# New order lists for the five engine queues of a fused attention and channel-mix kernel

## The chip, the cores and the metric

The kernel runs on one core of one Trainium2 chip. The metric is the device time of one execution in microseconds (us); lower is better. Runs are compared by their medians. The profile is one further execution, recorded instruction by instruction.

## The reference

Inputs are q, k and v of shape (8 batches, 8 heads, 576 tokens, 64), two mixing vectors and three weight matrices, all float32. The first half is causal attention in a window of 128 tokens with a linear penalty per head. Its result, laid out as (8, 576, 512), is x of the second half, a channel mix with a one-token shift.

```
scores = q @ k.T / 8 - slope[h] * (i - j),  only for 0 <= i - j < 128
x      = softmax(scores) @ v                        # then (batch, token, head*64 + d)
x_prev = x shifted by one token, zero at the start of a batch
xk     = mu_k * x + (1 - mu_k) * x_prev             # xr likewise with mu_r
k      = relu(xk @ w_k)                             # 512 -> 1024
out    = sigmoid(xr @ w_r) * ((k * k) @ w_v)        # 1024 -> 512
```

## The kernel before

The work is cut into 32 pairs of heads (8 batches of 4 pairs) for the attention, and into 4 pairs of batches (P = 0 to 3, 1152 tokens each) for the channel mix. Everything is written as named operations. The lists of names below (ORDER, from line 724) fix the order of the operations on each of five queues: PE (matmuls), ACT, DVE, POOL and SP. An engine takes its list in order: when one operation waits, all behind it on that engine wait too.

**Attention, pair n** (names end in the pair's number; pairs 0 to 3 are the first batch):

- `lql`, `lqp`, `lqn`, `lts` (POOL) load q and k; `lvs.b.j` loads V of batch b (j = 4 is the 64-token tail). `lts` loads the 64-token tails of q (0) and k (1). `lq` (SP) loads the first pair in float32.
- For batches 0 to 3, `ct` (DVE) reorders q and k by token, `tq` (PE) transposes them, `pq` (ACT) copies the result out of PSUM. The first pair has `c`, `tk` and `pk` as well. `tail` and `tcopy` do the same for the tails.
- For batches 4 to 7 the transposing is done by DMA instead: `tr.b.0` and `tr.b.1` (SP, line 92) cross all of q and of k of a batch, `trt` (line 97) its tails. `tr.b.i` needs the four loads `lqn.b.i.0` to `lqn.b.i.3`; the loads `lqn.(b+2).i.j` in turn go into the buffer that `tr.b.i` reads.
- `score.n.h` (PE, line 218) are the score matmuls of half h of the window, two heads side by side on 64 rows each. `exp` (ACT, line 226) takes the exponential, `mask` (DVE) multiplies by the window and penalty. The first four pairs add the penalty by an extra matmul (line 197) and have no `mask`.
- `av.n` (PE, line 249) multiplies by V and the row sum, `norm` (DVE, lines 260 and 261) divides, `ot` (PE) transposes back, `xt` (ACT) copies to the x tile. Pairs 0 to 3 do this in two halves, named `.0` and `.1`.
- `xk` and `xr` (DVE) make the two mixes.

**Channel mix, token chunks.** `m1.P.c0.f` (PE, line 312) is one 128-row slice f of xk @ w_k for the tokens from c0 on; a chunk has 256, 384 or 512 tokens. For two slices at the start it is split into `m1a` and `m1`. `rl` (ACT) is the relu, `kk` the square (DVE, twice in eight on ACT). `m3.P.c` (PE) is xr @ w_r for 128 tokens, `rs` (ACT) its gate. `m2a.P.c` and `m2.P.c` (PE) are the two halves of k*k @ w_v, `oo` (DVE) the product with the gate, `st` (SP) the store. The last two token blocks are split in columns instead (`oob`, `stb`). `lwk`, `lwr` and `lwv` (POOL) load the weights.

**Rings.** Tiles come from rings; an operation that takes a tile waits until the tile's users of one turn before are done. PSUM has a ring of 4 (`mm`: tq, tail, ot, m1, m3, m2a and the early av) and a ring of 2 (`sa`: scores and the later av). SBUF has 3 tiles for rl and 4 for the output product.

**Start.** `fill` are matmuls on zeros. `mask0` (ACT) computes the window mask, `mcopy` (DVE) copies it to its further places, `dcopy` and `sid` prepare the early pairs' penalty. `clear0`, `ms` and `clear` (POOL) are memsets: `clear0` for the first batch's V and k tails, `ms` for columns of the at and x tiles, `clear` for the other V buffers. The end is the last `oob` and `stb`.

How a list becomes dependences, and the crossbar with the planner's costs:

```
 568  op(("tr", b, i), "SP", 6800, lambda i=i: cross(b, i),
 569     [("lqn", b, i, j) for j in range(NF)] + old, n, land=9000)
 ...
 RINGS = {"sa": 2, "mm": 4, "ct": 3, "xu": 3, "dl": 4, "xm": 3, "xk": 2, "rl": 3,
          "kk": 2, "rs": 6, "ot": 4}
 ...
 for text in ORDER.values():
     line = [tuple(int(x) if x.isdigit() else x for x in w.split(".")) for w in text.split()]
     for a, o in zip(line, line[1:]):
         ops[o]["after"] = [a]
 plan()
```

`plan` emits the operations one after another; the `after` entries hold it to the lists. Its costs do not change what an engine executes or in which order.

Of the kernel before, what the change touches and what calls it, by code (L numbers as in the profile page):

```python
# [16 lines left out]
def kernel(  # L17
# [703 lines left out]
    for i, m in enumerate(FILL):  # L721
# [23 lines left out]
            m1.1.0.5 m1.1.0.7 av.15 m3.1.3 m3.1.0 score.19.1 score.19.0 ot.15 m1.1.0.3  # L745
            m3.1.1 m1.1.0.4 m1.1.0.1 m1.1.0.2 m1.1.512.0 m3.1.2 av.16 m1.1.512.5
            m2a.1.0 m1.1.512.3 m2a.1.2 m2.1.0 m1.1.512.4 av.17 av.18 m2.1.2 m1.1.512.1
            ot.16 m1.1.512.2 m1.1.512.6 m2a.1.3 score.21.1 score.20.1 m2.1.3 m3.1.6
            ot.18 score.22.1 score.22.0 m2a.1.1 ot.17 m2.1.1 av.19 m1.1.512.7 m3.1.5
            score.21.0 score.20.0 m3.1.8 m1.1.896.0 m3.1.4 m1.1.896.2 m3.1.7 ot.19  # L750
            score.23.0 score.23.1 m1.1.896.5 m1.1.896.7 m2a.1.6 m2a.1.4 m1.1.896.4
            m2.1.6 m2a.1.5 av.22 m2.1.4 m1.1.896.1 av.23 m2.1.5 ot.22 m1.2.0.0
            m1.1.896.3 m1.2.0.7 m1.2.0.1 av.20 m1.1.896.6 m1.2.0.6 m1.2.0.4 m1.2.0.3
            av.21 ot.20 m2a.1.8 m1.2.0.2 m2.1.8 ot.23 m3.2.1 m1.2.0.5 m3.2.0 ot.21
            m3.2.2 m2a.1.7 score.26.0 score.27.1 m2.1.7 m2a.2.0 m1.2.512.0 score.25.1
            score.24.1 m1.2.512.4 m2.2.0 m1.2.512.3 score.24.0 score.25.0 m3.2.3
            m1.2.512.6 score.26.1 score.27.0 m1.2.512.2 m1.2.512.7 m2a.2.3 m2a.2.1
            m2.2.3 m1.2.512.1 m2a.2.2 m2.2.1 m2.2.2 m1.2.512.5 m3.2.6 av.25 av.24
            m1.2.896.0 m3.2.4 av.27 m1.2.896.3 ot.24 m3.2.5 ot.27 ot.25 m1.2.896.7
            m2a.2.6 score.28.1 score.28.0 m3.2.8 m2a.2.5 av.26 m1.2.896.5 m2.2.6  # L760
            score.30.1 score.29.0 m2.2.5 m3.2.7 score.30.0 score.29.1 ot.26 m1.2.896.1
            m2a.2.4 av.28 m2.2.4 m1.2.896.4 m1.2.896.6 m1.3.0.0 m1.2.896.2 score.31.1
            score.31.0 m1.3.0.7 m1.3.0.3 m1.3.0.2 m1.3.0.1 av.30 ot.28 m2a.2.8
            m1.3.0.5 ot.30 m2.2.8 av.29 m1.3.0.6 m1.3.0.4 m3.3.1 m2a.2.7 m3.3.3 m2.2.7
            av.31 m3.3.2 ot.29 m3.3.0 m2a.3.2 ot.31 m2.3.2 m2a.3.0 m2a.3.3 m2a.3.1
            m2.3.0 m2.3.3 m1.3.512.0 m2.3.1 m1.3.512.3 m1.3.896.0 m1.3.512.4
            m1.3.896.6 m1.3.512.7 m3.3.4 m1.3.896.4 m1.3.896.3 m3.3.8 m1.3.512.1
            m1.3.512.2 m1.3.512.5 m1.3.896.5 m1.3.896.2 m1.3.896.1 m3.3.7 m3.3.5
# [7 lines left out]
            rl.0.0.0 rl.0.0.3 pq.7 rl.0.0.5 rl.0.256.0 rl.0.0.2 exp.5.1 rl.0.0.6
            rl.0.0.4 rl.0.256.5 rl.0.0.1 exp.7.0 rl.0.256.7 exp.6.0 rl.0.256.3
            rl.0.256.2 rl.0.0.7 rl.0.256.4 xt.4 rl.0.256.6 exp.7.1 pq.8 rl.0.256.1
            pq.9 xt.5 rs.0.0 rs.0.3 exp.8.1 xt.6 rs.0.2 exp.8.0 pq.10 rs.0.1 xt.7
            exp.9.0 exp.10.1 rl.0.512.0 rl.0.512.5 exp.9.1 rl.0.512.4 rl.0.512.7 pq.11  # L780
            kk.0.512.5 exp.10.0 rl.0.512.3 rl.0.768.0 xt.8 rl.0.768.1 exp.11.1 pq.12
# [19 lines left out]
            exp.29.1 rl.2.896.4 rl.3.0.0 rl.2.896.6 rl.2.896.2 rl.3.0.7 exp.31.1
            rl.3.0.3 rl.3.0.2 rl.3.0.1 exp.31.0 rl.3.0.5 xt.28 rl.3.0.6 xt.30 rl.3.0.4
            rs.3.3 rs.3.1 rs.3.2 xt.29 rs.3.0 xt.31 rl.3.512.0 rl.3.512.3 rl.3.512.4
            rl.3.896.0 rl.3.512.7 rl.3.896.6 rs.3.4 rl.3.896.4 rl.3.896.3 rs.3.8
            rl.3.512.1 rl.3.512.2 rl.3.512.5 rl.3.896.2 rl.3.896.5 rs.3.7 rl.3.896.1
            rs.3.5 rl.3.512.6 rs.3.6 rl.3.896.7
# [207 lines left out]
```

## Time and profile before

| | |
|---|---|
| median of 3 runs | 235.07 us (234.64 to 236.03) |
| the profiled execution, its own time | 235.28 us |
| its span, first to last instruction | 233.5 us |
| PE busy | 222.2 us, 95% |
| DVE busy | 192.6 us, 82% |
| ACT busy | 163.7 us, 70% |
| POOL busy, issuing loads and memsets | 93.1 us, 40% |
| granted TensorE clock | 0.999 |

Busy times of matmuls overlap, since they are pipelined, and their ends are modelled. "Idle before, releaser" means what the engine was waiting for. A DMA has two times, that of the instruction which issues it and that from the issue to its landing.

### The profile page before, as it was taken

How to read it: one execution, taken by the hardware profiler on the slowest of the kernel's cores; microseconds unless marked ns; L12 is line 12 of the kernel's file. 1: busy time of each engine (PE TensorE's matmuls, PEld its weight loads, DVE VectorE, ACT ScalarE, POOL GpSimd, SP SyncE). 2: the span in 40 equal slices, each digit the busy share in tenths (PEclk: the TensorE clock that was granted, in tenths of full speed). 3: DMA queues.
4: the chain of work that ended last, by engine and by line, in shares of the span. 5: the costliest groups of instructions: out<-in, count | busy, mean ns of one | idle time of the engine just before them, and what ended most of it. 6: DMA issues, size and time to landing. Idle time of an engine off the chain costs nothing.

```text
span 233.5 us, 5421 instructions
## 1 busy us (share of the span) xinstructions
PE 222.2 (95%) x2130; PEld 132.7 (57%) x2163; DVE 192.6 (82%) x406; ACT 163.7 (70%) x281; POOL 93.1 (40%) x131
## 2 busy tenths in 40 slices
...
GB/s 124 172 152 182 181 147 179 196 151 166 154 146 178 164 194 165 142 199 147 171 148 178 158 135 160 152 157 169 194 4 45 0 4 135 48 13 121 0 118 156
DMA packets 114810, 31.56 MB, mean 135 GB/s; under 512 B 99160, under 2 KB 110432, under 8 KB 114784
## 3 DMA queue, kind: packets, MB, share of 16 engines
...
q8 instruction: 17, 0.28, 0.6%
...
## 4 chain that ended last, share of the span: by engine, by line
PE 83%; POOL 9%; DMA 5%; issue 1%; ACT 0%; DVE 0%; POOLq 0%
PE ps L312 25%; PE pv L350 25%; PE pr L335 13%; PE sa L249 7%; PE sa L218 6%; DMA vs<-in_v_dram 5%; PE tp L269 4%; POOL vs L109 2%; POOL ql L129 2%; PE tp L157 2%; PE pv L357 2%; POOL ts L123 1%; POOL tv L440 1%; POOL wk_sb L422 1%; POOL ql L118 1%
## 5 line engine op out<-in xcount | busy, mean ns | idle before, releaser
L312 PE MATMUL ps<-xk,wk_sb 128*128 128x256 bf16 (+2 forms) x415 | 73.0, 314 | 0.7 <-DVE xk L301 0.3
L318 ACT ACTIVATE rl<-ps 128x256 bf16<-128x256 f32 (+2 forms) x104 | 47.7, 482 | 34.9 <-PE ps L312 30.5
L226 ACT ACTIVATE at<-sa 128x1024 bf16<-128x1024 f32 x64 | 65.7, 1051 | 7.5 <-PE sa L218 7.4
L350 PE MATMUL pv<-wv_sb,kk 128*128 128x512 bf16 x256 | 64.4, 379 | 1.1 <-issue 0.3
L312 PEld LDWEIGHTS <-wk_sb 128*128 128x128 bf16 x416 | 38.5, 98 | 24.5 <-issue 1.6
L231 DVE TENSOR_TENSOR at<-at,mask 128x1024 bf16<-128x1024 bf16 x56 | 37.8, 685 | 2.7 <-ACT at L226 2.6
L350 PEld LDWEIGHTS <-kk 128*128 128x128 bf16 x272 | 25.1, 98 | 24.8 <-issue 0.8
L335 PE MATMUL pr<-wr_sb,xr 128*128 128x512 bf16 x131 | 35.3, 379 | 0.6
L365 DVE SCALAR_TENSOR_TENSOR ot<-rs,pv 128x512 f32<-128x512 bf16 (+1 forms) x38 | 24.7, 655 | 13.0 <-PE pv L350 9.6
L327 DVE TENSOR_TENSOR kk<-rl 128x256 bf16<-128x256 bf16 (+2 forms) x88 | 27.6, 335 | 8.9 <-ACT rl L318 8.7
L109 POOL DMA_DIRECT2D vs<-in_v_dram x32 | 29.3, 925 | 6.9 <-DMA wv_sb<-in_moe_w_v_dram 4.3
L301 DVE SCALAR_TENSOR_TENSOR xk<-dl,mu_sb,xt 128x576 bf16<-128x576 bf16 (+2 forms) x36 | 27.1, 752 | 1.3
...
L341 ACT ACTIVATE rs<-pr 128x512 bf16<-128x512 f32 x36 | 22.3, 630 | 4.9 <-PE pr L335 4.8
L301 DVE SCALAR_TENSOR_TENSOR xr<-dl,mu_sb,xt 128x576 bf16<-128x576 bf16 x32 | 25.6, 812 | 0.0
L249 PEld LDWEIGHTS <-at 128*128 128x128 bf16 x576 | 21.5, 98 | 6.4 <-issue 1.1
L274 ACT COPY xt<-tp 128x576 bf16<-128x576 bf16 (+2 forms) x36 | 21.6, 606 | 4.2 <-PE tp L269 4.0
L261 DVE TENSOR_TENSOR xu<-sa,rc 128x640 bf16<-128x640 f32 x28 | 23.1, 824 | 1.0
L335 PEld LDWEIGHTS <-xr 128*128 128x128 bf16 x144 | 13.3, 98 | 12.3 <-issue 0.6
L249 PE MATMUL sa<-vs,at 128*128 128x65 bf16 x448 | 19.1, 194 | 1.0 <-DMA vs<-in_v_dram 1.0
L137 ACT COPY qk<-tp 128x1024 bf16<-128x1024 bf16 (+1 forms) x16 | 15.1, 942 | 6.0 <-PE tp L157 4.9
L294 DVE TENSOR_TENSOR dl<-xt 128x576 bf16<-128x576 bf16 (+2 forms) x36 | 15.1, 419 | 1.6 <-ACT xt L274 1.5
...
## 6 DMA issues: line engine op xcount, KB each, us to landing
out_dram<-ot SPq DMA_DIRECT2D x34, 256.0 KB, 2.9
...
ql<-in_q_dram POOLq DMA_DIRECT2D x7, 256.0 KB, 5.7
ql<-in_k_dram POOLq DMA_DIRECT2D x7, 256.0 KB, 6.9
wk_sb<-in_moe_w_k_dram POOLq DMA_DIRECT2D x2, 512.0 KB, 8.6
wv_sb<-in_moe_w_v_dram POOLq DMA_DIRECT2D x2, 512.0 KB, 11.2
```

Source lines behind the costliest of these rows:

```text
L109: nc.gpsimd.dma_start(out=vs_buf[b % NLD][:, j, :, 0:D], in_=v[b, :, 128 * j:128 * j + 128, :].rearrange("h p d -> p h d"))
L226: nc.scalar.activation(out=at_half(it, e), in_=T.pop(("sa", it, e)), func=AF.Exp, scale=float(scale))
L231: nc.vector.tensor_tensor(out=at_half(it, e), in0=at_half(it, e), in1=mask[:, 2 * g:2 * g + 2, 256 * e:256 * e + 512], op=ALU.mult)
L249: nc.tensor.matmul(pa[:, hl, W * (t - t0):W * (t - t0) + W], lhsT=at[:, lo:lo + 128], rhs=vs[:, u, 2 * g + hl, :] if u < NF else tvb[:, 2 ...
L261: nc.vector.tensor_tensor(out=xu[:, t0:t1].rearrange("p t h d -> p h t d"), in0=a5[:, :, :, 0:D], in1=rc[:, :, 0:n, None].to_broadcast([12 ...
L301: nc.vector.scalar_tensor_tensor(out=to, in0=T["dl", it][:, c0:c1], scalar=mu_sb[:, NPO * which + g:NPO * which + g + 1], in1=xp, op0=ALU. ...
L312: nc.tensor.matmul(ps[:, 0:c1 - c0], lhsT=wk_sb[:, po, 128 * fo:128 * fo + 128], rhs=xk[:, po, c0:c1], start=(po == 0), stop=(po == NPO - 1))
L318: nc.scalar.activation(out=rl[:, 0:c1 - c0], in_=T.pop(("ps", P, c0, fo))[:, 0:c1 - c0], func=AF.Relu, scale=RELU_SCALE)
L327: nc.vector.tensor_tensor(out=T["kk", P, c0][:, fo, 0:c1 - c0], in0=rl[:, 0:c1 - c0], in1=rl[:, 0:c1 - c0], op=ALU.mult)
L335: nc.tensor.matmul(pr, lhsT=T["xr", P][:, po, 128 * c:128 * c + 128], rhs=wr_sb[:, po], start=(po == 0), stop=(po == NPO - 1))
L350: nc.tensor.matmul(pv, lhsT=kk[:, fo, o:o + 128], rhs=wv_sb[:, fo], start=(fo == 0), stop=(fo == NFO - 1))
L365: nc.vector.scalar_tensor_tensor(out=T["ot", P, c][:, w0:w1], in0=T["rs", P, c][:, w0:w1], scalar=1.0, in1=pv[:, 0:w1 - w0], op0=ALU.add, ...
```

## The change

All five lists are replaced; nothing else is. Each holds the same names as before (PE 375, ACT 276, DVE 318, POOL 112, SP 58), so the operations, tile sizes, rings and costs in the code are untouched. The POOL list up to the loads of batch 6, the SP list up to the fifth batch's crossbar, and the parts of PE's and DVE's lists that the prediction speaks of:

```diff
         "PE": """
-            fill.0 fill.1 tk.0 tq.0 score.0.0 tmu tq.3 tail.0 tq.2 score.0.1 score.2.0
-            tq.1 score.2.1 av.0.0 av.2.0 score.3.0 ot.0.0 ot.2.0 av.0.1 av.2.1
...
-            score.5.1 m1.0.0.2 m1.0.256.0 score.7.0 m1.0.0.6 m1a.0.0.1 m1.0.0.4
-            m1.0.256.5 m1.0.0.1 av.4 m1.0.256.7 tail.2 m1.0.256.3 score.6.0 score.7.1
-            m1.0.256.2 m1.0.0.7 m1.0.256.4 m1.0.256.6 ot.4 av.5 tq.8 m1.0.256.1 tq.9
-            m3.0.0 av.6 ot.5 m3.0.3 score.8.1 score.8.0 ot.6 m3.0.2 tq.10 m3.0.1 av.7
-            m2a.0.1 m2a.0.0 score.9.0 score.10.1 ot.7 m2.0.1 m2a.0.3 m2.0.0 m2.0.3
...
-            av.12 m2a.0.4 av.13 m2.0.4 tq.15 ot.12 m2a.0.8 score.15.0 score.17.0
-            m2a.0.6 m1.1.0.0 av.14 m2.0.6 score.15.1 score.18.0 m2.0.8 m1.1.0.6
-            score.18.1 score.16.1 m2a.0.7 ot.14 m2.0.7 ot.13 score.16.0 score.17.1
...
-            m1.3.512.6 m3.3.6 m2a.3.4 m1.3.896.7 m2.3.4 m2a.3.5 m2a.3.6 m2.3.5 m2a.3.7
-            m2.3.6 m2.3.7 m2a.3.8 m2.3.8
+            fill.0 tq.0 tmu fill.1 tk.0 score.0.0 tail.0 tq.2 tq.3 score.0.1 tq.1
+            score.3.0 av.0.0 score.1.0 ot.0.0 av.3.0 score.2.0 ot.3.0 av.1.0 score.2.1
...
+            m1.0.0.3 score.6.0 m1.0.256.0 m1.0.0.5 m1.0.256.1 m1.0.256.4 score.5.1
+            score.7.0 m1.0.0.4 m1.0.256.3 m1.0.256.2 m1.0.256.5 m1.0.256.6 score.6.1
+            m1.0.256.7 score.7.1 m3.0.0 tail.2 m3.0.1 m3.0.3 m3.0.2 tq.9 m1.0.0.6 av.4
+            tq.8 m1.0.0.7 av.5 ot.4 av.6 tq.10 av.7 ot.5 tq.11 tail.3 score.8.1 ot.6
+            score.8.0 ot.7 m2a.0.0 m2a.0.1 score.9.0 score.9.1 m2.0.1 m2.0.0 m2a.0.2
...
+            m1.0.768.2 av.13 score.14.0 m1.1.0.0 m1.0.768.5 ot.13 av.12 m1.1.0.3
+            m1.1.0.6 m2a.0.7 av.14 score.15.0 m2.0.7 score.16.0 score.18.1 ot.12
+            m1.1.0.4 av.15 m1.1.0.5 m2a.0.8 score.19.0 score.18.0 ot.15 ot.14 m2.0.8
+            m1.1.0.2 score.17.1 score.16.1 m3.1.0 m1.1.0.1 m2a.0.6 m1.1.0.7 m3.1.2
...
+            m1.3.896.4 m2.3.6 m1.3.896.3 m2a.3.4 m2a.3.5 m1.3.896.7 m2.3.4 m2.3.5
+            m3.3.8 m2a.3.7 m2a.3.8 m2.3.7 m2.3.8
         """,
         "DVE": """
-            sid c.0.0 dcopy c.0.1 pk.0 mcopy.1 id8 mcopy.2 ct.3 cmu ct.2 tcopy.0 pk.2
-            ct.1 mcopy.0 pk.3 pk.1 norm.0.0 norm.2.0 xk.0.0 norm.0.1 norm.2.1 xk.2.0
...
-            ct.8 kk.0.256.2 xr.3 ct.9 mask.6.0 kk.0.0.7 norm.5 norm.6 kk.0.256.1
-            mask.7.1 ct.10 mask.7.0 xk.4 xk.5 kk.0.256.6 norm.7 xk.6 kk.0.256.4 xr.5
+            dcopy c.0.0 sid c.0.1 id8 pk.0 cmu ct.2 ct.3 tcopy.0 pk.2 ct.1 pk.3 pk.1
+            norm.0.0 mcopy.0 norm.3.0 mcopy.1 norm.1.0 ct.4 xk.0.0 mcopy.2 norm.2.0
...
+            norm.4 ct.10 norm.5 ct.11 norm.6 norm.7 kk.0.0.6 kk.0.0.7 tcopy.3 xk.4
...
+            norm.9 mask.10.1 mask.11.1 ct.14 kk.0.512.6 kk.0.768.6 ct.15 norm.11
         """,
         "POOL": """
-            clear0 lql.0.1.0 lql.0.1.1 lts.0.1 lts.0.0 lqp.1.1 lqp.1.0 ms lvs.0.0
-            lvs.0.1 lvs.0.3 lvs.0.2 lvs.0.4 lql.1.0.0 lql.1.0.1 lts.1.0 lts.1.1
-            lql.1.1.1 clear lql.1.1.0 lwk.0 lwk.1 lvs.1.1 lvs.1.0 lvs.1.3 lvs.1.2
-            lvs.1.4 lts.2.1 lts.2.0 lql.2.0.1 lql.2.0.0 lwr lvs.3.4 lql.2.1.0
-            lql.2.1.1 lwv.0 lwv.1 lts.3.1 lvs.2.4 lts.3.0 lql.3.1.1 lvs.2.2 lvs.2.1
-            lvs.2.3 lvs.2.0 lql.3.0.1 lql.3.0.0 lqn.4.1.3 lql.3.1.0 lvs.3.3 lvs.3.2
-            lqn.4.0.1 lqn.4.0.3 lqn.4.1.2 lqn.4.0.0 lqn.4.0.2 lts.5.1 lts.4.1 lvs.3.1
-            lqn.4.1.1 lts.4.0 lqn.4.1.0 lvs.3.0 lqn.6.1.3 lvs.4.3 lqn.5.0.0 lqn.5.0.3
...
+            lql.0.1.1 lql.0.1.0 lts.0.1 lts.0.0 lqp.1.0 clear0 lqp.1.1 lvs.0.0 lvs.0.1
+            lql.1.0.0 lql.1.0.1 lts.1.1 ms lts.1.0 lvs.0.3 lvs.0.2 lvs.0.4 lql.1.1.0
+            lql.1.1.1 lwk.0 clear lql.2.0.1 lwk.1 lql.2.0.0 lts.2.1 lwr lts.2.0
+            lvs.1.4 lvs.1.0 lvs.1.2 lvs.1.1 lvs.1.3 lql.2.1.0 lql.2.1.1 lts.3.1
+            lts.3.0 lwv.0 lwv.1 lvs.2.3 lql.3.0.0 lts.4.1 lql.3.1.1 lvs.2.1 lql.3.0.1
+            lvs.2.0 lvs.2.2 lvs.2.4 lqn.4.1.3 lvs.3.4 lqn.4.1.0 lql.3.1.0 lvs.3.1
+            lqn.4.1.1 lvs.3.0 lqn.4.0.3 lqn.4.0.1 lts.4.0 lqn.4.1.2 lvs.4.1 lqn.4.0.2
+            lqn.5.1.3 lqn.4.0.0 lvs.3.3 lvs.3.2 lqn.5.1.0 lqn.5.0.1 lqn.6.0.2
+            lqn.5.0.0 lqn.5.1.2 lqn.6.0.3 lqn.5.1.1 lvs.4.3 lvs.4.0 lvs.4.2 lqn.5.0.2
+            lqn.5.0.3 lvs.4.4 lts.5.0 lts.5.1 lqn.6.1.1 lts.6.0 lqn.6.1.0 lts.7.0
+            lvs.7.0 lvs.5.2 lqn.6.0.1 lqn.6.1.2 lqn.6.0.0 lqn.6.1.3 lvs.5.0 lvs.5.1
...
         """,
         "SP": """
-            lq.0.0 lq.0.1 lmu.0 lmu.1 tr.4.0 st.0.1 st.0.0 tr.4.1 trt.4.0 st.0.3
-            trt.4.1 st.0.5 st.0.2 st.0.8 tr.5.0 st.0.4 trt.5.1 tr.5.1 trt.5.0 st.0.7
...
+            lq.0.0 lq.0.1 lmu.1 lmu.0 st.0.0 trt.4.0 trt.4.1 st.0.1 tr.4.1 tr.4.0
+            st.0.3 st.0.2 st.0.4 st.0.5 tr.5.1 st.0.8 trt.5.0 st.0.7 trt.5.1 st.0.6
+            tr.5.0 st.1.2 st.1.0 st.1.1 tr.6.0 st.1.3 tr.6.1 st.1.6 trt.6.1 trt.6.0
...
         """,
```

In the new POOL list five loads (`lql.0.1` twice, `lts.0` twice, `lqp.1.0`) stand ahead of `clear0`, and `ms` moves behind the third load of batch 1 (`lts.1.1`). On PE, an unbroken run of scores is a stretch of the list with nothing but `score` names; from pair 4 on the old list has 31 of them and the new one 33.

More of the change, by code (lines that the diff above doesn't have):

```diff
@@ L744 @@
-            score.18.1 score.16.1 m2a.0.7 ot.14 m2.0.7 ot.13 score.16.0 score.17.1
[L745 to L768, printed above, removed]
@@ L769 @@
-            m1.3.512.6 m3.3.6 m2a.3.4 m1.3.896.7 m2.3.4 m2a.3.5 m2a.3.6 m2.3.5 m2a.3.7
-            m2.3.6 m2.3.7 m2a.3.8 m2.3.8
+            fill.0 tq.0 tmu fill.1 tk.0 score.0.0 tail.0 tq.2 tq.3 score.0.1 tq.1
+            score.3.0 av.0.0 score.1.0 ot.0.0 av.3.0 score.2.0 ot.3.0 av.1.0 score.2.1
+            av.2.0 score.3.1 tq.4 tail.1 score.1.1 av.0.1 ot.2.0 ot.1.0 av.2.1
+            score.4.1 av.1.1 tq.5 ot.0.1 score.4.0 ot.2.1 av.3.1 ot.1.1 score.5.0
+            ot.3.1 tq.7 tq.6 m1a.0.0.0 m1.0.0.0 m1a.0.0.1 m1.0.0.1 fill.2 m1.0.0.2
@@ new lines @@
+            m1.0.0.3 score.6.0 m1.0.256.0 m1.0.0.5 m1.0.256.1 m1.0.256.4 score.5.1
[3 more added lines that the diff above has]
+            score.8.0 ot.7 m2a.0.0 m2a.0.1 score.9.0 score.9.1 m2.0.1 m2.0.0 m2a.0.2
+            score.10.1 score.11.0 m2.0.2 m1.0.512.0 m2a.0.3 m1.0.512.1 m2.0.3
@@ new lines @@
+            m2a.2.5 score.30.1 score.31.0 m2.2.4 m2.2.5 av.29 m1.3.0.0 m1.2.896.3
+            av.28 m1.3.0.7 m1.3.0.5 m1.3.0.2 m1.2.896.7 m3.2.7 m1.3.0.3 m2a.2.8
+            m1.3.0.4 m2.2.8 m1.3.0.1 av.30 ot.29 m3.3.3 m3.3.2 m1.3.0.6 ot.28 av.31
+            ot.30 m3.3.1 m2a.2.7 m3.3.0 m2.2.7 ot.31 m2a.3.2 m2a.3.3 m2a.3.0 m2.3.2
+            m2.3.0 m2.3.3 m2a.3.1 m1.3.512.0 m2.3.1 m1.3.512.3 m1.3.512.1 m1.3.512.5
+            m1.3.512.6 m1.3.512.2 m1.3.896.0 m3.3.5 m3.3.7 m1.3.512.4 m1.3.896.6
@@ L776 @@
[L776 to L781, printed above, removed]
@@ L801 @@
[L801 to L806, printed above, removed]
+            mask0.4 pq.0 mask0.6 mask0.0 exp.0.0 pq.2 mask0.2 pq.3 exp.0.1 pq.1
@@ new lines @@
+            kk.1.896.4 kk.2.0.3 kk.2.0.2 norm.21 mask.20.1 kk.1.896.2 kk.1.896.3
+            norm.23 norm.22 kk.2.0.7 norm.20 xk.21 kk.2.0.4 xk.20 xk.22 xk.23 xr.21
+            mask.25.0 oo.1.8 oo.1.7 kk.2.0.6 mask.27.0 xr.20 oo.2.0 xr.22 mask.25.1
+            mask.26.1 mask.24.1 mask.27.1 mask.24.0 kk.2.512.3 oo.2.1 norm.25 norm.24
+            kk.2.512.0 oo.2.3 norm.27 xr.23 mask.26.0 kk.2.512.6 kk.2.512.7 oo.2.2
+            xk.24 kk.2.896.0 kk.2.512.2 norm.26 kk.2.512.4 mask.29.0 xk.27 oo.2.6
```

162 lines of the change are left out of this document (88 added, 74 removed).

## The prediction

> **What bounds the kernel now.** I read the page first, then busy time by stretches, then the waits. First row below: the page's busy time; next four: stretches of the span (length, then busy us of PE, PEld, DVE, ACT, POOL, granted clock, DMA share, GB/s); last two: waits (total, times, longest).
>
> ```profile
> PE 222.2 (95%) x2130; PEld 132.7 (57%) x2163; DVE 192.6 (82%) x406; ACT 163.7 (70%) x281; POOL 93.1 (40%) x131
> ...
> 0.00:20.00 20.00, 16.63 (x179) 8.82 (x182) 16.11 (x49) 14.13 (x25) 19.04 (x42) 1.00 1.45 151
> 20.00:40.00 20.00, 17.31 (x236) 13.05 (x234) 18.45 (x49) 18.05 (x34) 12.35 (x17) 1.00 1.80 174
> 40.00:60.00 20.00, 19.79 (x212) 12.57 (x214) 19.28 (x40) 16.36 (x27) 13.39 (x16) 1.00 1.66 170
> ...
> 220.00:233.50 13.50, 10.02 (x64) 6.08 (x63) 4.71 (x11) 1.56 (x4) 0.00 (x0) 0.97 0.32 118
> ...
> PE sa L249 <- DMA vs<-in_v_dram: 1.0, 1, 1.0
> ...
> PEld L218 <- issue: 9.5, 26, 0.4
> ```
>
> PE is the bound, and nearly closed up. Of its 11.3 us idle (233.5 - 222.2), 3.4 lie in the first stretch, 2.7 in the second and 3.5 at the end, where the last product and store follow the last matmul. That leaves 1.7 us for 40 to 220. A new order can win only in the first 40 us; anywhere it can lose. In that head DVE is full too (18.45 and 19.28 of 20), and so is DMA.
>
> The chain of waits (start, length, what) names the load at which the head last stops PE, V of batch 1 for av.4. It also gives the times of later operations and the prices of matmul groups:
>
> ```profile
> 22.03 12.25 DMA vs<-in_v_dram
> ...
> 38.52 0.28 PE tp L269 x5
> ...
> 39.34 0.45 PE tp L157 x8
> ...
> 43.23 0.55 PE sa L218 x12
> ...
> 45.47 0.86 PE pr L335 x4
> 46.33 0.55 PE sa L249 x18
> ...
> 49.81 3.19 PE pv L350 x14
> ...
> 55.19 0.87 PE ps L312 x8
> ...
> 59.71 0.65 PE ps L312 x4
> ...
> 62.76 0.55 PE sa L249 x18
> ...
> 91.76 0.55 PE sa L218 x12
> ```
>
> In the order list these are ot.4 (0.28, any ot), tq.8 (0.45), score.8.1 with 8.0 (0.55 for a pair's two halves), m3.0.1 (0.86; m2 runs at the same rate), av.7 (0.55), m2.0.1, two 256-wide m1 (0.43 each), a 384-wide m1 (0.65), av.9, and score.16.0 with 17.1. A tail is 0.3 (four of tq's eight transposes, rounded up).
>
> **The first loads.** The change only reorders five lists; every operation and every matmul stays. POOL's timeline, a wr row of the list of issues, and two looks at single loads:
>
> ```profile
> 0.84 0.34 POOL L389 IOTA dist<- 128x256 bf16 x1 [0.39 <-POOLq L998]
> 1.23 0.53 POOL L440 MEMSET tv<- 64x520 bf16 x1
> ...
> 2.25 0.90 POOL L129 DMA_DIRECT2D ql<-in_q_dram  x1
> ...
> 6.78 0.43 POOL L891 MEMSET at<- 128x64 bf16 x4
> ...
> 7.20 3.55 POOL L109 DMA_DIRECT2D vs<-in_v_dram  x4
> ...
> 31.67 0.74 POOL L427 DMA_DIRECT2D wr_sb<-in_moe_w_r_dram  x1 [0.99 <-DMA vs<-in_v_dram]
> wr_sb<-in_moe_w_r_dram POOLq DMA_DIRECT2D x1, 512.0 KB, 8.2
> ...
> 35.32 0.75 POOL L129 DMA_DIRECT2D ql<-in_k_dram  x1
> DMA to landing us min/median/max: 8.2/8.2/8.2
> ...
> 36.05 1.50 POOL L427 DMA_DIRECT2D wv_sb<-in_moe_w_v_dram  x2
> DMA to landing us min/median/max: 10.0/11.2/12.4
> ```
>
> Today clear0 (1.23 to 2.25) stands ahead of the first load; now five loads go first, so the first is issued 1.0 us earlier. But clear0 then delays those behind it: up to lvs.0.0 POOL has the same work less ms (6.78 to 7.20), now behind five more loads. So the shift that lasts is between 0.4 us (POOL's sum) and 1.0 us (first issue). I take 0.4, since the V loads were POOL's to issue at 0.9 each.
>
> The later landings follow by comparing which loads stand ahead. lvs.1.3, the last V of batch 1, has ahead of it exactly the loads that wr had: 31.67 + 8.2 - 0.4 = 39.5. lql.2.1.1 loses only the 64 KB lvs.3.4 ahead (0.4 at 174 GB/s): 35.32 + 8.2 - 0.4 - 0.4 = 42.7. lwv.1 (issued 36.8, landed 49.2) loses lvs.3.4 and gains two 64 KB tails: 49.2 + 0.4 - 0.4 = 49.2.
>
> **When PE asks for them.** I take the old time and correct it for matmuls that changed sides. av.4 was due about 33.0 and stopped until the 34.28 at which the first chain row ends. Ahead of it now come also six 256-wide m1 (2.6), four m3 (3.4), two score halves (0.55), a tail and tq.9 (0.75): 33.0 + 7.3 = 40.3, against 39.5. m2.0.1 gains tq.11 and tail.3: 49.81 + 0.75 = 50.6, against 49.2. av.7 loses score.8.0, 8.1, ot.5 and ot.6, about 1.3 with the edges below: 45.0. For it DVE's durations count:
>
> ```profile
> 34.98 0.22 DVE L260 RECIPROCAL rc<-sa 128x10 f32<-128x10 f32 x1 [1.20 <-PE sa L249]
> 35.23 0.82 DVE L261 TENSOR_TENSOR xu<-sa,rc 128x640 bf16<-128x640 f32 x1
> ...
> 38.24 0.42 DVE L148 COPY ct<-ql 128x1024 bf16<-128x1024 bf16 x1
> ```
>
> A norm is 1.07 us, a ct 0.42. In DVE's new list ct.10, which waits for lql.2.1.1, stands ahead of norm.5; behind it queue ct.11, norm.6 and norm.7. av.7 takes the PSUM tile that norm.5 frees. So: landing 42.7, ct.10 to 43.1, norm.5 to 44.2, av.7 at 44.35 at the earliest, 0.65 ahead of 45.0. From there ct.11 and norm.6 bring norm.7 to 45.5 and its end to 46.6; score.8.0 needs that tile at 43.5 + 3.7 = 47.2 (m3.0.1, m3.0.2, tq.10, tq.11, tail.3, av.7, ot.6). The smallest room is 0.6 us. PE may come to m3.0.0 earlier than that, since three mask copies (mcopy) leave DVE's list ahead of the first norms and fill its waits. What is gained there beyond 0.6 us is waited for again at these tiles. Term: **-0.6**, bounds 0 (DVE, full in both orders, gives nothing) and -1.2 (with the 1.0 us shift).
>
> **Score edges.** Scores load 64-row weights, everything else 128-row ones:
>
> ```profile
> 151.17 0.81 PE L312 MATMUL ps<-xk,wk_sb 128*128 128x384 bf16 x4
> 151.91 0.34 PE L218 MATMUL sa<-qt 64*128 64x256 bf16 x4
> 152.34 0.19 PE L218 MATMUL sa<-tt 64*128 64x64 bf16 x2
> 152.47 0.34 PE L312 MATMUL ps<-xk,wk_sb 128*128 128x384 bf16 x1
> ...
> L226 ACT ACTIVATE at<-sa 128x1024 bf16<-128x1024 f32 x64 | 65.7, 1051 | 7.5 <-PE sa L218 7.4
> ```
>
> Four 384-wide matmuls from 151.17 would be through at 151.82 (0.65), the scores begin at 151.91; their last two 64-wide ones from 152.34 take 0.03, m1 begins at 152.47. Each unbroken run of scores costs 0.09 + 0.10. From pair 4 on the old list has 31 runs, the new one 33: **+0.4**.
>
> The Trainium skill (TensorE: Matmul & The Clock Gate, Step-by-step: what each phase is for) says that weight loads are pulled ahead of running matmuls, if they go to the background buffer or other row groups. By that rule the edges would be free and this term 0; the wait row of L218 (9.5 us, 26 times) does not agree, and the sum goes by the rows.
>
> **PSUM for scores.** Two tiles rotate. In the new list score.18.1 takes the tile of score.15.0 with only m2.0.7 and score.16.0 between, 0.86 + 0.3 us, where exp alone is 1.05 and a hand-over about 0.2. Likewise score.16.0 follows av.14 by 1.3, a norm with its hand-overs. I put **+0.2** for both (bounds 0 and 0.6: DVE's queue ahead of norm.14).
>
> **Costed at nothing.** The tail: m2.3.4, m2.3.5 and m3.3.8 (2.6 us) stand between the last m1 and m2a.3.7, and cover its rl and kk, under 1 us; without that cover it would cost that. SP: trt.4.0, trt.4.1 and tr.4.1 now stand ahead of st.0.3, st.0.2, and oo.0.7 waits for st.0.2's buffer; its place is behind m2.0.7, over 5 us after that store can go. POOL: lvs.7.0 waits for av.16 to av.19, with lvs.5.x queued behind; av.21 asks for those more than 15 us of matmuls after av.19.
>
> **Sum.** -0.6 + 0.4 + 0.2 = 0. The profiled execution took 235.28 us (span 233.5 and 1.8 around it), 0.2 above the median of 235.07, so the forecast is 235.3 on its scale and **235.1** as median: no change. About 0.5% (1.2 us) is what a measurement of this kernel can tell from none.
>
> **Rival, faster.** The head keeps its lead: loads come 1.0 us earlier, DVE's gap-filling mask copies let PE run up to that, and the edges and PSUM waits fall into it. For it: 6.1 us of idle in the first 40, only part of it start-up. Against: DVE full from 20 on. Price -1.2 to -2.0; I put 233.5.
>
> **Rival, slower: the crossbar before score.16.0.** SP's rows of line 92, with its times to landing:
>
> ```profile
> 66.78 4.16 SPq L92 DMA_TRANSPOSE qt<-ql  x1
> ...
> 126.35 14.26 SPq L92 DMA_TRANSPOSE qt<-ql  x2
> ...
> DMA to landing us min/median/max: 4.3/5.1/12.9
> ```
>
> Today tr.4.0 is issued at 66.78, when its last load is in. Now four 128 KB loads (0.9) and two tails (0.75) more stand ahead of that: 71.5, and lqn.5.1.3 among them waits for ct.15, a few DVE operations behind norm.9 (av.9 at 62.76 + 0.8), which I estimate at 3 us: 74.5. tr.4.1 goes first, near 69. score.16.0 is due at 91.76 less 4.2 (four m2, four scores and two ot go behind it, one m1 ahead) = 87.5. With the median landing tr.4.0 is in by 80, 7 us of slack. But two crossbars among queued loads took 14.26 to issue, and a landing up to 12.9 behind the second, some 7 into the pair: 69 + 20 = 89 to 90, PE stopped for 2.3. This decides from a landing over 13 us on. For it: 126.35. Against: POOL soon stands at lqn.6.0.2, which waits for tr.4.0, so the queue empties. The same lateness reaches lvs.3.3 and lvs.3.2 for av.13, up to 1 us. 237.4.
>
> The Trainium skill (DMA: Bandwidth & Descriptors, Queues, rings and completion order) lets each engine take turns between queues packet by packet, so a transfer on SP's queue slows with what POOL has queued; the 4.16 and 14.26 agree.
>
> **Rival: it doesn't do what it says.** The planning costs in the code are untouched; if the lists bring no earlier load, the lead is 0 and the edges remain: 235.7.
>
> **Chances.** No change as summed 0.37; faster 0.28; crossbar or V late 0.25; no lead 0.10, of which a third over 0.5%, and 0.04 of the first case falls there too. Faster 0.28, within 0.5% 0.39, slower 0.33. The likeliest case spans 234.2 to 236.0 by its terms' bounds; the range takes in most of both rivals: 233.2 to 237.5.
>
> **What would show it.** First load at 1.2 us; PE at m3.0.0 near 35 to 36; ct.10 waiting for a ql load near 42.7; av.7 near 44.4; 33 runs of scores; PE waits on qt none. A wait of PE over 1 us behind 50 us, on qt, vs or a norm, would make it wrong upwards; PE over 1.2 us ahead at score.8.0 and still so at 200, downwards.

## The result, and the profile after

The changed kernel took 236.06 us in the median (235.33 to 237.78), the kernel before 235.18 (234.25 to 236.46) in the same comparison: a ratio of 1.0043, 95% interval 1.0023 to 1.0064 (the two medians alone give 1.0037; all ratios here lie nearer to those of the means). That is 0.4% slower, within the 0.5% that the forecast called no change, and inside its range of 233.2 to 237.5. But the sum came near by other terms than its own. The profiled execution took 236.05 us, with a span of 234.3.

Busy time by stretches of the changed kernel (columns as before):

```profile
0.00:20.00 20.00, 15.41 (x140) 7.56 (x141) 14.23 (x42) 12.61 (x22) 18.88 (x41) 1.00 1.50 156
20.00:40.00 20.00, 18.47 (x233) 13.10 (x231) 19.58 (x54) 19.41 (x36) 14.12 (x19) 1.00 1.85 184
40.00:60.00 20.00, 19.85 (x246) 13.47 (x245) 19.43 (x38) 16.70 (x27) 14.94 (x20) 1.00 2.03 178
```

In the first 20 us PE did 1.2 us less (16.63 before) and DVE 1.9 us less (16.11). The head, which was to win 0.6, begins late. In the second stretch PE does 1.2 more than before (17.31): most of the delay is made up there, because V of batch 1 no longer stops av.4 (1.80 us from its start to that of the next operation in the kernel before, 0.55 now).

The chain of waits names both places where the change lost time (start, length, what):

```profile
3.66 6.36 DMA ts<-in_q_dram
...
69.08 1.75 POOL ql L87 x2
71.68 8.64 DMA vs<-in_v_dram
```

The waits (total, times, longest) have the same two, and the edges of the scores:

```profile
PEld L218 <- issue: 10.9, 29, 0.4
...
POOL ql L87 <- DVE ct L148: 7.0, 1, 7.0
...
PEld L170 <- DMA ts<-in_k_dram: 1.8, 1, 1.8
PE to L170 <- DMA ts<-in_q_dram: 1.6, 1, 1.6
```

**The head.** L170 is tail.0. It now stands ahead of tq.2 and tq.3 on PE and waits for a 64 KB load, which was issued at 3.66 instead of 4.57 and yet landed at 10.03 instead of 9.13. Behind it hangs a chain over three engines; the timelines of PE, DVE and ACT (start, length, what, in brackets the idle time before):

```profile
10.16 0.38 PE L170 MATMUL to<-ident,ts 128*128 128x128 bf16 x4 [1.57 <-DMA ts<-in_q_dram]
...
14.22 0.39 PE L218 MATMUL sa<-qk 64*128 64x256 bf16 x4 [1.03 <-DVE qk L134]
```

```profile
10.58 0.42 DVE L176 COPY tt<-to 128x512 bf16<-128x512 bf16 x1 [0.48 <-PE to L170]
11.03 0.69 DVE L134 COPY qk<-tp 128x512 bf16<-128x512 bf16 x1
...
13.47 1.29 DVE L134 COPY qk<-tp 128x512 bf16<-128x512 bf16 x2 [1.42 <-ACT qk L137]
```

```profile
11.75 0.59 ACT L137 COPY qk<-tp 128x512 bf16<-128x512 bf16 x1 [2.10 <-DVE qk L134]
12.24 0.72 ACT L414 ACTIVATE mask<-dist 128x256 bf16<-128x256 bf16 x2
12.86 0.58 ACT L137 COPY qk<-tp 128x512 bf16<-128x512 bf16 x1
```

tail.0 at 10.16, tcopy.0 (L176), behind it on DVE pk.2 (11.03), for it pq.2 on ACT (11.75), mask0.2, pq.3, for that pk.3 (13.47), and for that score.3.0 on PE (14.22). In the kernel before, the transposes of pair 3 stand ahead of tail.0, and tail.0 finds its load landed.

**V for av.13.** POOL issues nothing for 7.0 us at lqn.5.1.3, which waits for ct.15. Behind it are lqn.4.0.0, lvs.3.3 and lvs.3.2. POOL's timeline, and PE's at av.13:

```profile
61.20 0.88 POOL L87 DMA_DIRECT2D ql<-in_q_dram  x1 [0.33 <-DMA vs<-in_v_dram]
69.08 0.88 POOL L87 DMA_DIRECT2D ql<-in_k_dram  x1 [7.01 <-DVE ct L148]
69.95 0.88 POOL L87 DMA_DIRECT2D ql<-in_q_dram  x1
70.81 1.77 POOL L109 DMA_DIRECT2D vs<-in_v_dram  x2
...
80.36 0.40 PE L249 MATMUL sa<-vs,at 128*128 128x65 bf16 x8 [0.23 <-DMA vs<-in_v_dram]
```

lvs.3.2 landed at 71.68 + 8.64 = 80.32, and av.13 could go on. From its first matmul to that of the next operation, score.14.0, av.13 took 1.03, where it takes 0.64 in the kernels below that have its V in time: 0.39 lost. In this execution that is little, because PE was late anyway. It is also a ceiling: no PE that is earlier could pass av.13 before 80.3.

**PE against the kernel before.** To compare kernels whose lists differ I take for each operation its start on PE less the median durations (start to start, by kind, from the trace of before) of all that stands ahead of it in its own list. The difference between two kernels at the same sum of work is the lag below; minus is a lead. At 10 to 15 us of work the changed kernel lags by up to 1.8, at 24 (with the V wait of before behind it) by 0.19, at 64 by 0.34, at 80 (past av.13) by 0.83, at the end by 0.77. In the head such a figure depends by some tenths on how the medians of its few operations are taken; the differences between kernels hardly do.

### The profile page after: what moved, and what is told of

It reads as the page before. It is cut to its first block, busy times and chain, and to the rows that moved or that the text cites. A ratio compares the mean times of both kernels' runs of the same rounds, so it can differ in the third digit from the quotient of the medians.

```text
span 234.3 us, 5451 instructions
## 1 busy us (share of the span) xinstructions
PE 224.3 (96%) x2163; PEld 133.0 (57%) x2163; DVE 193.4 (83%) x406; ACT 164.4 (70%) x281; POOL 93.4 (40%) x131
## 4 chain that ended last, share of the span: by engine, by line
PE 70%; DVE 16%; DMA 6%; POOL 2%; issue 2%; ACT 2%; POOLq 0%; DVEq 0%
PE pv L350 24%; PE ps L312 22%; PE pr L335 10%; PE sa L218 5%; PE sa L249 5%; DMA vs<-in_v_dram 4%; DVE at L231 4%; DMA ts<-in_q_dram 3%; PE tp L269 3%; DVE xu L261 3%; DVE ct L148 2%; DVE xk L301 2%; PE pv L357 1%; DVE kk L327 1%; DVE qk L134 1%
## 5 line engine op out<-in xcount | busy, mean ns | idle before, releaser
L226 ACT ACTIVATE at<-sa 128x1024 bf16<-128x1024 f32 x64 | 64.4, 1033 | 9.6 <-PE sa L218 9.4
L318 ACT ACTIVATE rl<-ps 128x256 bf16<-128x256 f32 (+2 forms) x104 | 46.1, 472 | 33.1 <-PE ps L312 27.0
L350 PE MATMUL pv<-wv_sb,kk 128*128 128x512 bf16 x272 | 66.6, 379 | 0.0
L231 DVE TENSOR_TENSOR at<-at,mask 128x1024 bf16<-128x1024 bf16 x56 | 37.1, 684 | 1.2 <-ACT at L226 1.2
L327 DVE TENSOR_TENSOR kk<-rl 128x256 bf16<-128x256 bf16 (+2 forms) x88 | 27.8, 335 | 11.6 <-ACT rl L318 11.4
L109 POOL DMA_DIRECT2D vs<-in_v_dram x32 | 28.3, 897 | 22.2 <-PE sa L249 11.4
L335 PE MATMUL pr<-wr_sb,xr 128*128 128x512 bf16 x144 | 36.2, 379 | 0.0
L341 ACT ACTIVATE rs<-pr 128x512 bf16<-128x512 f32 x36 | 21.4, 603 | 9.5 <-PE pr L335 9.3
L274 ACT COPY xt<-tp 128x576 bf16<-128x576 bf16 (+2 forms) x36 | 21.1, 599 | 4.0 <-PE tp L269 4.0
L87 POOL DMA_DIRECT2D ql<-in_q_dram x16 | 14.3, 904 | 14.8 <-DMA qt<-ql 12.0
```

Of the source, the lines that this page charges most:

```text
L87: nc.gpsimd.dma_start(out=qn_buf[b % 2][:, i, j].rearrange("p (h d) -> p h d", h=H), in_=(q, k)[i][b, :, 128 * j:128 * j + 128, :].rearran ...
L109: nc.gpsimd.dma_start(out=vs_buf[b % NLD][:, j, :, 0:D], in_=v[b, :, 128 * j:128 * j + 128, :].rearrange("h p d -> p h d"))
L226: nc.scalar.activation(out=at_half(it, e), in_=T.pop(("sa", it, e)), func=AF.Exp, scale=float(scale))
L231: nc.vector.tensor_tensor(out=at_half(it, e), in0=at_half(it, e), in1=mask[:, 2 * g:2 * g + 2, 256 * e:256 * e + 512], op=ALU.mult)
L318: nc.scalar.activation(out=rl[:, 0:c1 - c0], in_=T.pop(("ps", P, c0, fo))[:, 0:c1 - c0], func=AF.Relu, scale=RELU_SCALE)
L327: nc.vector.tensor_tensor(out=T["kk", P, c0][:, fo, 0:c1 - c0], in0=rl[:, 0:c1 - c0], in1=rl[:, 0:c1 - c0], op=ALU.mult)
```

## The experiments

All edits only move names in the lists. C is clear0 first on POOL, T tail.0 one step later, M the mask activations earlier on ACT, V the loads lvs.3.x ahead of lqn.5.1.3. Lag of PE at 24 and 64 us of work (before V is asked for), at 80 and at the end, from the one profiled execution of each; medians and ratios from the executions of its comparison. The kernel before was measured again beside them: its median was 235.18 for the changed kernel, 235.37 for the next three rows, 235.51 for V and the last two, 235.17 for the two between.

| kernel | lag at 24 | 64 | 80 | end | median us | ratio to before (95%) |
|---|---|---|---|---|---|---|
| changed kernel | +0.19 | +0.34 | +0.83 | +0.77 | 236.06 | 1.0043 (1.0023 to 1.0064) |
| C | -0.20 | -0.20 | -0.10 | -0.17 | 235.55 | 1.0020 (0.9996 to 1.0043) |
| T, M | -1.14 | -0.88 | +0.75 | +0.70 | 236.16 | 1.0033 (1.0011 to 1.0054) |
| C, T, M | -1.67 | -1.48 | +0.50 | +0.44 | 234.30 | 0.9975 (0.9948 to 1.0001) |
| V | -0.43 | -0.18 | -0.08 | -0.15 | 235.47 | 1.0013 (0.9989 to 1.0037) |
| C, V | +0.18 | +0.61 | +0.71 | +0.63 | 234.98 | 0.9994 (0.9974 to 1.0013) |
| T, V | -1.24 | -1.20 | -1.10 | -1.18 | 235.04 | 0.9983 (0.9966 to 1.0001) |
| C, T, V | -1.46 | -1.10 | -1.00 | -1.07 | 234.31 | 0.9960 (0.9938 to 0.9983) |
| C, T, M, V | -1.39 | -1.30 | -1.20 | -1.27 | 234.38 | 0.9959 (0.9940 to 0.9978) |

### clear0 first again (C)

```diff
-            lql.0.1.1 lql.0.1.0 lts.0.1 lts.0.0 lqp.1.0 clear0 lqp.1.1 lvs.0.0 lvs.0.1
+            clear0 lql.0.1.1 lql.0.1.0 lts.0.1 lts.0.0 lqp.1.0 lqp.1.1 lvs.0.0 lvs.0.1
```

> The changed kernel with clear0 back at the front of POOL's list; nothing else is edited. Theory A (the first loads): issued 0.9 us earlier they share the DMA engines with the first pair's float32 loads, so the k part lands at 5.05 instead of 4.23 and the q tail at 10.03 instead of 9.13. With clear0 first: the tail near 9.1 to 9.5, tail.0 on PE no longer waits 1.6, PE 0.7 to 1.0 us earlier at score.0.1, and what is left of it at the end 0.4 to 0.9: 235.2 to 235.6. Theory B (later causes: more unbroken runs of scores, late V for av.13; the head is given back before 25 us, as PE's lag fell from 1.8 to 0.2 there): the landings move as said, the time stays at 236.1 +- 0.3.

Measured: 235.55, ratio 1.0020. The first pair's k landed at 4.23, the q tail at 9.63, score.0.1 started at 10.88 (11.27 in the changed kernel). The ratio fell by 0.0023, 0.5 us; the two intervals overlap. It fits theory A, but not yet against chance.

### The same edit, reversed, on the kernel before

```diff
-            clear0 lql.0.1.0 lql.0.1.1 lts.0.1 lts.0.0 lqp.1.1 lqp.1.0 ms lvs.0.0
+            lql.0.1.0 lql.0.1.1 lts.0.1 lts.0.0 lqp.1.1 clear0 lqp.1.0 ms lvs.0.0
```

> The kernel before with clear0 moved behind its first five loads; nothing else is edited. Theory A: the same collision makes the first pair's k land near 5.0 and the q tail near 10, and PE in the first 20 us loses 0.5 to 1.0, of which 0.3 to 0.9 stays at the end: 235.5 to 236.1. Theory B: no change within 0.3 (235.1). The prediction's own step said 0.4 to 1.0 earlier loads and so up to 0.6 faster: 234.5.

Measured: 235.54 against 235.37, ratio 1.0005 (0.9989 to 1.0021). Here the early loads did land earlier, the first at 6.42 (6.96), the q tail at 8.75 (9.13): the 0.4 of the prediction's step. Nothing of it reached the end. Theory A's collision did not show in this kernel (k landed at 4.29), and the hope of 0.6 did not either.

### Three operations of the head (T and M)

```diff
         "PE": """
-            fill.0 tq.0 tmu fill.1 tk.0 score.0.0 tail.0 tq.2 tq.3 score.0.1 tq.1
+            fill.0 tq.0 tmu fill.1 tk.0 score.0.0 tq.2 tq.3 tail.0 score.0.1 tq.1
...
         "ACT": """
-            mask0.4 pq.0 mask0.6 mask0.0 exp.0.0 pq.2 mask0.2 pq.3 exp.0.1 pq.1
+            mask0.4 mask0.6 mask0.0 mask0.2 pq.0 exp.0.0 pq.2 pq.3 exp.0.1 pq.1
...
         "DVE": """
-            dcopy c.0.0 sid c.0.1 id8 pk.0 cmu ct.2 ct.3 tcopy.0 pk.2 ct.1 pk.3 pk.1
+            dcopy c.0.0 sid c.0.1 id8 pk.0 cmu ct.2 ct.3 pk.2 tcopy.0 ct.1 pk.3 pk.1
```

> The changed kernel with three moves in the head: on PE tail.0 behind tq.2 and tq.3, on DVE tcopy.0 behind pk.2, on ACT all of mask0 ahead of pq.0, where ACT waits 3.1 us anyway. The loads stay as they are. If the order of these few operations makes the head late (tail.0 waits 1.6 us for its load and holds tq.2; mask0.2 stands 0.7 us ahead of pq.3, for which DVE waits 1.4), PE reaches score.3.0's second part 1 to 1.5 us earlier and the end 0.4 to 1.0 earlier: 235.1 to 235.7. Theory B: 236.1 +- 0.3.

Measured: 236.16, ratio 1.0033, hardly better. By the time alone the theory would have fallen. The trace says otherwise: PE was 0.9 to 1.1 ahead of the kernel before from 24 to 64 us, and at av.13 lost all of it.

```profile
80.29 0.40 PE L249 MATMUL sa<-vs,at 128*128 128x65 bf16 x8 [1.38 <-DMA vs<-in_v_dram]
```

lvs.3.2 landed at 80.24, as in the changed kernel (80.32), while PE began av.13 at 78.53: the ceiling. The gain turned into a wait 60 us later.

### Head and clear0 together (C, T, M)

The edits of the two sections above on the changed kernel.

> The moves of the two experiments on the changed kernel together: clear0 first on POOL, tail.0 and tcopy.0 one step later, mask0 ahead of pq.0. If the lag of the head (0.4 at 50 us, against the 0.6 lead that was predicted) is the cause, all of it goes: PE at m2.0.1 near 49.3 to 49.7 and 234.9 to 235.4. If DVE, full from 20 us on, gives nothing, or the loss arises later, 236.1 +- 0.3.

Measured: 234.30, ratio 0.9975. In the profiled execution PE led by 1.5 until av.13 and lost 2.0 there:

```profile
67.44 0.88 POOL L87 DMA_DIRECT2D ql<-in_k_dram  x1 [5.74 <-DVE ct L148]
68.31 0.88 POOL L87 DMA_DIRECT2D ql<-in_q_dram  x1
69.17 1.77 POOL L109 DMA_DIRECT2D vs<-in_v_dram  x2
...
80.03 0.40 PE L249 MATMUL sa<-vs,at 128*128 128x65 bf16 x8 [1.72 <-DMA vs<-in_v_dram]
```

That execution took 235.71; the median is 1.4 below. In the profiled execution the two loads ran beside a crossbar (tr.4.1, issued at 68.78, landed at 81.02). That they are not as late every time is a guess; no trace of a faster execution shows it. But by its median this kernel has most of the gain without V.

### V ahead of the load that waits (V)

```diff
-            lqn.5.1.3 lqn.4.0.0 lvs.3.3 lvs.3.2 lqn.5.1.0 lqn.5.0.1 lqn.6.0.2
+            lqn.4.0.0 lvs.3.3 lvs.3.2 lqn.5.1.3 lqn.5.1.0 lqn.5.0.1 lqn.6.0.2
```

> The changed kernel with one name moved on POOL: lqn.5.1.3, which waited 7.0 us for ct.15, behind lqn.4.0.0, lvs.3.3 and lvs.3.2. Theory C (V held behind that wait stops PE at av.13): these three are issued near 62, 7 us earlier; lvs.3.2 lands near 69 to 72 instead of 80.3, av.13 loses its 0.56 and the time falls by 0.3 to 0.6: 235.4 to 235.8. tr.4.0 goes out near 70. Rival: av.13's excess is the score's or the norm's, and the time stays at 236.1 +- 0.3.

Measured: 235.47, ratio 1.0013, 0.7 us less than the changed kernel's ratio gives (0.0030 of 235). lvs.3.2 was issued at 64.93 and landed at 72.69, the wait for ct.15 shrank to 3.0 us, and PE loses 0.1 from 64 to 80 (-0.18, -0.08) where the changed kernel loses 0.5. The wait of theory C is gone. How much of the 0.7 is its doing is less sure: the two intervals overlap, and in the two traces 0.52 of the 0.92 between the lags at the end was there at 64, ahead of av.13.

### All three edits (C, T, M, V)

> The moves of the head (clear0 first; tail.0 and tcopy.0 one step later; mask0 ahead of pq.0) and lqn.5.1.3 behind lvs.3.2. In the profile of the head's moves PE was 1.4 us ahead of the kernel before up to 72 us and lost 1.95 waiting for V at av.13. Theory C: that wait is gone, the lead of 1.0 to 1.5 reaches the end, less 0.4 for edges: 233.6 to 234.3, ratio 0.992 to 0.996. Rival: V was only the first late load, the next one (a crossbar before score.16.0, or the exp queue) takes the lead back: 234.3 to 235.4.

Measured: 234.38, ratio 0.9959 (0.9940 to 0.9978), faster than both kernels. Against C, T, M the ratio fell by 0.0016, within the intervals, and the median hardly moved. In the trace, PE's 1.3 of lead at 64 us is there at the end. av.13 runs through, with its V in since 69.87:

```profile
67.73 1.75 POOL L87 DMA_DIRECT2D ql<-in_k_dram  x2 [3.57 <-DVE ct L148]
...
78.11 0.62 PE L249 MATMUL sa<-vs,at 128*128 128x65 bf16 x15
```

Nothing else took the lead back; both crossbars of batch 4 were in by 81.5. The rival fell.

### Which move of the head (C, T, V)

ACT's list as in the changed kernel, the rest as with all three.

> As the kernel with all three edits, but with ACT's list as in the changed kernel: mask0.2 again between pq.2 and pq.3. Tells the two moves of the head's order apart. If mask0.2 is what held DVE at pk.3 (1.4 us): 0.5 to 0.9 slower than with all three. If the place of tail.0 is: no difference within 0.3.

Measured: 234.31, ratio 0.9960: no difference. Beside C, T and V the place of mask0.2 is worth nothing, although it stands in the chain of the head: with tail.0 moved the chain is early enough. It is tail.0 and tcopy.0.

### tail.0 and V, loads early (T, V), and clear0 and V (C, V)

> The changed kernel with two edits: tail.0 on PE behind tq.2 and tq.3 with tcopy.0 behind pk.2, and lqn.5.1.3 behind lvs.3.2. The five loads stay ahead of clear0, ACT's list stays. Theory D (the place of tail.0 alone makes the head late: three transposes wait for the tail's load): nearly all of the gain of the three edits, 234.2 to 234.8, ratio 0.995 to 0.998. Theory A (the early loads): most of it missing, 235.0 to 235.6.

> The changed kernel with clear0 first on POOL and lqn.5.1.3 behind lvs.3.2; tail.0 stays ahead of tq.2. Theory D: little better than with lqn.5.1.3 alone, 235.0 to 235.6, since tail.0 still waits for its load, by some 0.4 less. Theory A: 234.2 to 234.8.

Measured: T, V 235.04, ratio 0.9983; C, V 234.98, ratio 0.9994. Neither theory gets all. By the ratios tail.0 is worth 0.0030 between V and T, V, and 0.0034 between C, V and C, T, V: 0.7 to 0.8 us both times. (With M it is 0.0010 on the changed kernel and 0.0045 beside C.) The clear0 edit is worth 0.0023, 0.0019 and 0.0023 in three pairs (alone, beside V, beside T and V), 0.5 us, and 0.0058 in a fourth, beside T and M. V is worth 0.0030, 0.0026 and 0.0016. All have one sign, but the two intervals of each pair overlap, save in that fourth. The medians, each over that of the kernel before, split the same gain otherwise: tail.0 0.0004 and 0.0043 in the two pairs, clear0 0.0030, 0.0006, 0.0045 and 0.0079, V 0.0039, 0.0016 and 0.0003. So the shares of the three edits are not settled. What both measures show is that C and T together, with or without V and M, give the three lowest rows of the table, and that about 0.008 lies between the changed kernel and the best. In the traces the head divides the kernels cleanly: all with T lead by 1.0 to 1.7 at 24 us, all without lie between -0.43 and +0.19.

What the move does, in the timelines with T and V of PE and of DVE:

```profile
9.14 1.37 PE L157 MATMUL tp<-ident,ct 128*128 128x128 bf16 x16 [0.34 <-DVE ct L148]
10.35 0.39 PE L170 MATMUL to<-ident,ts 128*128 128x128 bf16 x4
...
12.99 0.39 PE L218 MATMUL sa<-qk 64*128 64x256 bf16 x4 [0.15 <-DVE qk L134]
```

```profile
9.80 0.69 DVE L134 COPY qk<-tp 128x512 bf16<-128x512 bf16 x1
10.77 0.42 DVE L176 COPY tt<-to 128x512 bf16<-128x512 bf16 x1 [0.28 <-PE to L170]
```

tail.0 runs no earlier (10.35), but pk.2 begins at 9.80 instead of 11.03 and score.3.0's second part at 12.99 instead of 14.22: 1.2 us, the head's loss. With C and V alone, where q and k had landed by 8.16, PE still stood at tail.0 until 10.17 and score.3.0 came at 14.23.

### The order of q and k in the first loads

```diff
-            lql.0.1.1 lql.0.1.0 lts.0.1 lts.0.0 lqp.1.0 clear0 lqp.1.1 lvs.0.0 lvs.0.1
+            lql.0.1.0 lql.0.1.1 lts.0.1 lts.0.0 lqp.1.1 clear0 lqp.1.0 lvs.0.0 lvs.0.1
```

> As the kernel with tail.0 moved and V first, with the five early loads in the order of the kernel before: q ahead of k in the first two, lqp.1.1 ahead of clear0. In the kernel before with these five ahead of clear0 the first load landed at 6.42 and the q tail at 8.75; in the changed kernel, issued as early, at 7.78 and 10.03. If the order of q and k does it: first landing near 6.4, q tail near 8.8, time 0 to 0.5 lower than without this edit. If it is scatter from execution to execution, or what other engines do meanwhile: landings of 7.0 to 7.8 and 9.4 to 10.0, no change.

Measured: 234.92, ratio 0.9979 (0.9963 to 0.9994), against 0.9983 without the edit; first landing 6.92 (6.83), q tail 9.15 (9.05). The order does nothing. The changed kernel's 7.78 and 10.03 were not the order either: with the same POOL list up to there, T, V had 6.83 and 9.05. It is scatter from one execution to the next.

### The price of a run of scores

Based on all three edits; 13 runs of two scores are cut, for instance:

```diff
-            m1.1.0.2 score.17.1 score.16.1 m3.1.0 m1.1.0.1
+            m1.1.0.2 score.17.1 m3.1.0 score.16.1 m1.1.0.1
```

> As the kernel with all three edits, with 13 runs of two scores from batch 4 on cut in two by one m1, m2 or m3 (46 unbroken runs instead of 33); each of the second scores is 0.4 to 0.9 us later. By the prediction's price of 0.19 for each run: 2.5 us slower than with all three (1.9 if some of it was waited for anyway). By the rule that weight loads are pulled ahead: no change within 0.4.

Measured: 237.81, ratio 1.0092 (1.0058 to 1.0126), which is 3.1 us by the ratios and 3.4 by the medians above the kernel with all three edits, in six executions. Waits of this kernel, then of the one with all three edits:

```profile
PEld L218 <- issue: 15.2, 41, 0.4
...
PE sa L218 <- DMA qt<-ql: 0.7, 1, 0.7
```

```profile
PEld L218 <- issue: 11.3, 30, 0.4
```

Some 0.7 of it is one wait for a crossbar that the other kernel does not have. The rest, 2.4 to 2.7, is 0.18 to 0.21 for each cut; the steps of PE's lag in the two traces give 0.21. The price of 0.19 stands. The Trainium skill (TensorE: Matmul & The Clock Gate, Step-by-step: what each phase is for) says that weight loads are pulled ahead of running matmuls where the row groups do not conflict or the load goes to the background buffer. If one of the two held at these edges, the price would be 0; this measurement does not agree for these 64-row scores, and no run here shows which condition failed.

### Two runs fewer

```diff
-            ... m1.0.256.6 score.6.1 m1.0.256.7 score.7.1 ... tail.3 score.8.1 ot.6 score.8.0
+            ... m1.0.256.6 m1.0.256.7 score.6.1 score.7.1 ... tail.3 ot.6 score.8.1 score.8.0
```

> clear0 first, tail.0 and tcopy.0 one step later, lqn.5.1.3 behind lvs.3.2, ACT's list of the changed kernel, and two runs of scores fewer: score.6.1 behind m1.0.256.7, next to score.7.1, and score.8.1 behind ot.6, next to score.8.0. By 0.19 to 0.27 for each run 0.4 to 0.5 faster than without the last edit: 233.8 to 234.1. If the later exp of 6.1 is waited for: no gain, 234.2 to 234.5.

Measured: 234.53, ratio 0.9971 (0.9956 to 0.9986): no gain. PE came to m3.0.0 at 35.17 instead of 35.30 and gave it back at av.7, which waited for the tile of a norm:

```profile
43.56 0.63 PE L249 MATMUL sa<-vs,at 128*128 128x65 bf16 x15 [0.33 <-DVE xu L261]
```

That wait is absent without the edit. Where DVE sets the pace, a saved edge is not a saved microsecond.

## Why the prediction was right or wrong

It summed -0.6 (lead of the head), +0.4 (edges) and +0.2 (PSUM) to no change. Measured was +0.9 between the medians and +0.77 by PE's lag: 0.34 of it at 64 us of work, where the lead was to be, 0.49 more at av.13, and nothing after. That the total missed by no more than this was luck: a lead that did not come and a wait that was not in the sum, against edges and PSUM waits that do not show in the lag. The likeliest case was said to span 234.2 to 236.0; its terms' bounds (-0.8 and +1.0) give 234.3 to 236.1, and 236.06 lies at the top of it.

- **The lead of the head, -0.6: wrong.** At 24 us PE lagged by 0.19. The step that failed is the one that followed the first loads only as a shift of 0.4 to 1.0 on all later ones. I had tail.0 in the sum of matmuls by its duration, 0.3, and did not ask what it waits for in its new place ahead of tq.2. It waited 1.6, and a chain of copies waited with it, 1.2 us at score.3.0. The sign for the lead, m3.0.0 near 35 to 36, came out at 36.96. There was a lead to have: with tail.0 one step back and V in time it was 1.1 to 1.3 at the end in four of five kernels (0.8 in the fifth), about the bound of -1.2 that stood beside the term. But it did not come by the mechanism of the term, earlier first loads: it is as large with clear0 first, where the first load is issued at 2.25 as before. About as much as this lead is what all these kernels save at av.4, 1.25 us.
- **The shift of the loads: direction right, by luck.** The first load was issued at 1.34 (1.2 was forecast), and it landed no earlier. The later ones came earlier than I had worked out: lvs.1.3 at 38.60 (39.5), lql.2.1.1 at 40.51 (42.7), lwv.1 at 46.46 (49.2). It was not the shift that brought them: with clear0 first (C) they landed at 37.89, 39.82 and 45.85.
- **ct.10 waits for its load: wrong.** The load was in at 40.51; ct.10 began at 43.30, behind four masks on a DVE without a gap. Still PE met the tile where I had put it: score.8.0 waited 0.15 for a norm and started at 47.39, where 47.2 was forecast. The room of 0.6 at that tile did not cap the lead: in the kernels with T score.8.0 began 1.0 to 1.8 ahead of that 47.2, so their DVE was as much earlier. A full DVE handed an early start on as faithfully as a late one.
- **Edges, +0.4: the price is right**, 0.18 to 0.21 for each run measured where PE sets the pace, and so is the count of 33 runs. That the two more runs cost this kernel 0.4 is not shown: taking two away gained nothing.
- **PSUM, +0.2: not there.** From av.14's start to that of score.15.0 passed 0.64, as in every kernel with this order, and neither score.16.0 nor score.18.1 waited for a tile.
- **V for av.13: named, but in the wrong sum.** "Up to 1 us" stood in the slower rival, and nothing of it in the sum. It is 0.39 in the changed kernel and 1.5 to 1.9 where the head is early (T, M and C, T, M). The mis-sized term is POOL's wait at lqn.5.1.3: 7.0 us, not 3.
- **The crossbar before score.16.0: near.** tr.4.0 was issued at 78.57 (74.5) and landed at 85.50; score.16.0 started at 88.00, so 2.5 us of the 7 were left. On qt only the weight loads waited, 0.4. (The 71.5 in its sum comes out as 71.1 or 71.9, as the 0.75 is meant for both tails or for each; nothing hangs on it.)
- **Costed at nothing: right.** POOL waited 11.4 us at lvs.7.0 and 12.0 at lqn.6.0.2, and PE for neither.

The rival "it doesn't do what it says", 235.7, comes closest to what happened: no lead. The wait for V, 0.39, is about what is left.

**What stays open.** Why clear0 first is worth 0.5 us or more in four pairs, when the tail lands no later on average with the loads first, and when the same edit on the kernel before changes nothing. The traces do not help: at 64 us of work the kernel with clear0 first is ahead of its partner by 0.54 and 0.60 in two of the pairs (alone; beside T and M), and behind it by 0.79 and 0.10 in the other two (beside V; beside T and V).
